# A fused attention and wave-MLP kernel: attention in fine stages, one written order for three batches

## The chip, the cores and the metric

One core of one Trainium2 chip. The metric is the device time of one execution in microseconds (us), as the median of the runs. Five engines work side by side, each on its own queue: TensorE (PE in the profile; PEld is its weight load), VectorE (DVE), ScalarE (ACT), GpSimd (POOL) and SyncE (SP), which here issues all the transfers.

## The reference

Eight batches, eight heads, 576 tokens, head size 64. First an attention in two parts, then a channel and token mixer on its output.

```python
q_d, k_d, v_d = (t.reshape(B, H, 144, 4, D).mean(axis=3) for t in (q, k, v))
out_up = np.repeat(softmax(q_d @ k_d.T / 8) @ v_d, 4, axis=2)      # pooled attention
scores = np.where(abs(pos[:, None] - pos[None, :]) < 4, q @ k.T / 8, -1e9)
out_local = softmax(scores) @ v                                     # band of seven tokens
x = (out_up + out_local).transpose(0, 2, 1, 3).reshape(B, 576, 512)

theta = x @ w_theta
y = einsum('ts,bsd->btd', w_tok_r, x * cos(theta)) + einsum('ts,bsd->btd', w_tok_i, x * sin(theta))
u = x + y
out = u + maximum(u @ w_ch, 0)
```

## The kernel before

All matmuls are in bf16 with float32 sums; the inputs arrive as float32 and are cast on the chip. The batches run one after another as a software pipeline written by hand. Every stage is a Python generator that emits a few instructions and then yields:

- `load(b)` (L78) issues the transfers of q, k and v on SP's queue, in pieces. `cast(b)` (L126) turns them into bf16, on GpSimd but for the first batch's queries. The float32 and the bf16 buffers exist once each, v in bf16 twice.
- `attention(b)` (L278) is one generator for the whole attention. Its eight turns (L294) bring q and k into the layout with the head dimension on partitions, one pair of heads at a time, with the pooling as 24 more columns of the same matmul; ScalarE copies the 576 turned columns and VectorE the 144 pooled ones. For the first two batches (`WIDE`) q and k arrive in another layout and a turn has twelve matmuls. Then come the pooled values (L336), three steps of pooled scores with their exponentials (L354), five steps of scores, each with an exponential on ScalarE and two masking passes on GpSimd (L388), two of pooled output (L423), mixed in among the scores, and five of output (L461). An output step upsamples the pooled result by a matmul with a staircase matrix (`RT`; two matmuls where a chunk of 120 tokens lies on the border of the two halves of 72 pooled rows, six in a batch), multiplies the masked scores with v, and makes a chunk of x on VectorE (reciprocal, product `tmp`, sum `x`).
- `modulate(b)` (L503) transposes x, multiplies by w_theta, takes cosine and sine on ScalarE (a table of its own, so the engine reloads its table twice a batch) and multiplies by x on VectorE (`z`).
- `mix(b)` (L545) has eight steps of token mix and five of channels. In the token mix the two halves of the 576 tokens are built side by side in two banks; after 20 matmuls VectorE adds x to both. A channel step multiplies by w_ch, transposes u back, applies the rectifier on ScalarE (`rel`), adds on VectorE (`osb`) and stores.
- `build_WT` (L241) loads, casts and transposes the two token matrices, within the first batches.

The order of the work comes from the string `PERIOD` (L610): in iteration b it takes steps of attention b+1 (a), modulation b (m) and mix b-1 (x) in turn. Each attention itself emits the loads and casts of the next batch (`next(loads, 0)`, `ahead()`). The first attention is emitted alone ahead of the loop. The framework that places the instructions may still reorder what is emitted within an engine, by priorities of its own; it also sets the semaphores.

PSUM has eight banks: tiles of two banks with two buffers (`w2`: turns, scores, pooled scores and outputs) and tiles of one bank with four (`w1`: pooled values, upsampling, transposes, phases, mix, channels).

Of the kernel before, what the change touches and what calls it, by code (L numbers as in the profile page):

```python
# [13 lines left out]
P = 128  # L14
# [31 lines left out]
def kernel(  # L46
# [31 lines left out]
    def load(b):  # L78

        ts = staged[b] = []  # L80
        for nm in "qk":
            ts.append(work.tile([TR, NTR * H * D], FP32, tag=f"{nm}32", bufs=1, name=f"{nm}32_{b}"))
        if b < WIDE:
            for hh in range(4):
                for t, src in zip(ts, (q, k)):
                    nc.sync.dma_start(
                        out=t.rearrange("p (h e) -> p h e", h=H)[:, 2 * hh:2 * hh + 2, :],
                        in_=src[b, 2 * hh:2 * hh + 2].rearrange("h (p r) d -> p h (r d)", r=NTR),
                    )
                    yield  # L90
        else:
            for t, src in zip(ts, (q, k)):
# [7 lines left out]
        t = work.tile([P, NCH, H, D], FP32, tag="v32", bufs=1, name=f"v32_{b}")  # L100
        ts.append(t)
# [21 lines left out]
    kdT = const.tile([P, 4, 180], BF16, name="kdT")  # L123
    nc.vector.memset(kdT[:, :, SD:180], 0.0)

    def cast(b, engines):  # L126

        q32, k32, v32 = staged.pop(b)
# [4 lines left out]
        if b < WIDE:  # L133
            for hh in range(4):
                for eng, dst, src in ((engines[0], q_tm, q32), (engines[1], k_tm, k32)):
                    eng(out=dst[:, :, 2 * hh:2 * hh + 2, :].rearrange("p r h d -> p h r d"),
                        in_=src.rearrange("p (h r d) -> p h r d", h=H, d=D)[:, 2 * hh:2 * hh + 2])
                    if hh % 2 == 0 or eng is engines[1]:
                        yield
        else:  # L140
            for eng, dst, src in ((engines[0], q_tm, q32), (engines[1], k_tm, k32)):
                for c in range(0, NTR, 2):
                    eng(out=dst[:, c:c + 2], in_=src.rearrange("p (c h d) -> p c h d", c=NTR, d=D)[:, c:c + 2])  # L143
                    yield
        engines[2](out=v_w[:, 0:2, :, 0:D], in_=v32[:, 0:2])
        yield
        engines[2](out=v_w[:, 2:4, :, 0:D], in_=v32[:, 2:4])
        yield
        engines[2](out=v_w[0:KW[4], 4, :, 0:D], in_=v32[0:KW[4], 4])
# [21 lines left out]
    pw = moep.tile([TR, NTR, SD], BF16, tag="rel", bufs=3, name="pw")  # L171
# [14 lines left out]
    for _ in range(6):  # L186
# [39 lines left out]
    for c in range(4):  # L226
# [3 lines left out]
    ru = const.tile([72, 288 + S], BF16, name="ru")  # L230
    nc.vector.memset(ru, 1.0)
    nc.gpsimd.affine_select(out=ru, in_=ru, compare_op=ALU.is_ge, fill=0.0,
                            base=-288, pattern=[[1, 288 + S]], channel_multiplier=-4)
    nc.gpsimd.affine_select(out=ru, in_=ru, compare_op=ALU.is_ge, fill=0.0,
                            base=291, pattern=[[-1, 288 + S]], channel_multiplier=4)
    RT = [ru[:, 288 - 288 * g:288 - 288 * g + S] for g in range(2)]
# [4 lines left out]
    def build_WT():  # L241
        w_tm = [moep.tile([P, 5, S], BF16, tag="uT", name=f"wtm{ri}") for ri in range(2)]
        pieces = []
        for ri, w_dram in enumerate((moe_w_tok_r, moe_w_tok_i)):
            for ct in range(5):
                t = moep.tile([P, S], FP32, tag=("osb", "rel")[ct % 2], bufs=3, name=f"wt32_{ri}{ct}")
                rows = OC[ct]
                nc.sync.dma_start(out=t[0:rows], in_=w_dram[P * ct:P * ct + rows, :])
                pieces.append((w_tm[ri][0:rows, ct, :], t[0:rows]))
                if len(pieces) == 5:  # L250
                    yield
                if len(pieces) > 5 or ri:
                    dst, src = pieces.pop(0)
                    nc.gpsimd.tensor_copy(out=dst, in_=src)
        nc.sync.dma_start(out=w32[1], in_=moe_w_ch.rearrange("(c p) e -> p c e", p=P))
        yield
        for dst, src in pieces:
            nc.gpsimd.tensor_copy(out=dst, in_=src)
            yield
        for c in range(4):  # L260
            nc.gpsimd.tensor_copy(out=wch[:, c, :], in_=w32[1][:, c, :])
# [12 lines left out]

    xs = {}


    def attention(b):  # L278
        q_tm, k_tm, v_w = inputs.pop(b)
        loads = load(b + 1) if b + 1 < B else iter(())  # L280
        casts = []

        def ahead(n=1):
            if b + 1 < B:
                if not casts:
                    casts.append(cast(b + 1, (nc.gpsimd.tensor_copy,) * 3))
                for _ in range(n):
                    next(casts[0], 0)

        qT = work.tile([P, 4, S], BF16, tag="qT", bufs=1, name=f"qT{b}")  # L290
        kT = work.tile([P, 4, S], BF16, tag="kT", bufs=1, name=f"kT{b}")
        qdT = work.tile([P, 4, SD], BF16, tag="qdT", bufs=1, name=f"qdT{b}")

        def turn(n, hh):  # L294
            tm, To, Tdo = ((q_tm, qT, qdT), (k_tm, kT, kdT))[n]
# [366 lines left out]
```

## Time and profile before

| what | value |
|---|---|
| median of 3 runs | 335.38 us (335.3 to 335.72) |
| the profiled execution | 336.12 us |
| its span, first to last instruction | 334.4 us |
| mean granted TensorE clock | 0.923 |
| busy: TensorE, weight loads | 294.0 us (88%), 204.9 us (61%) |
| busy: VectorE, ScalarE, GpSimd | 195.0, 186.0, 159.2 us (58, 56, 48%) |
| moved by DMA | 43.57 MB, mean 130 GB/s |

Busy times are sums of instructions' durations, overlaps counted once. A row of a timeline has a start, a length, an engine, a line of the kernel, an operation, what it writes and reads, how many instructions are merged, and in brackets the idle time before it with what ended it. Matmuls are pipelined: the length of a merged row runs past the start of the next one, so the cost of a group is read from one start to the next. The granted clock is given as a share of full speed, a mean over the stretch of the two levels 1.2 and 2.4 GHz.

### The profile page before, as it was taken

To read this page: it belongs to the slowest core of one execution; us is meant where nothing else is said; L and a number is where in the kernel's file an instruction comes from. 1 tells how busy PE (TensorE), PEld (TensorE's weight loads), DVE (VectorE), ACT (ScalarE), POOL (GpSimd) and SP (SyncE) were. 2 spreads that over 40 slices of the span, in tenths; PEclk is the share of its full clock that TensorE was granted. 3 is DMA by queue.
4 is the path that set the end of the run, shared out by engine and by line. 5 is a ranking of instruction groups with operands and counts; after the bars stand their busy time and mean duration, and the time that the engine had idled before them with its cause. 6 is when DMAs were issued, how large, how long until landed. Compare 5 with 4: busy or idle time off the path is not lost.

```text
span 334.4 us, 7314 instructions
## 1 busy us (share of the span) xinstructions
PE 294.0 (88%) x2940; PEld 204.9 (61%) x2954; DVE 195.0 (58%) x441; ACT 186.0 (56%) x280; POOL 159.2 (48%) x186
## 2 busy tenths in 40 slices
PE   1688898999996899979997899889998999699994
PEld 1664685576664676557664666566755766467672
DVE  5426846594546764685439664766466544934533
ACT  1264289424874668628872787377855596333302
POOL 6977504893049524964477447815790008300000
PEclk9995589558999999979999999999998999979999
DMA  8999999959302289639917895477012000300303
GB/s 221 235 321 218 234 285 228 200 92 201 77 2 90 62 142 206 143 104 204 194 38 212 153 209 101 142 176 142 2 65 78 2 0 14 117 16 2 136 7 141
DMA packets 107826, 43.57 MB, mean 130 GB/s; under 512 B 97424, under 2 KB 101520, under 8 KB 107792
## 3 DMA queue, kind: packets, MB, share of 16 engines
q1 hardware_dynamic: 107792, 43.10, 58.6%
q8 instruction: 23, 0.38, 0.5%
q14 instruction: 11, 0.09, 0.1%
HBM read 33.65 MB, written 9.44 MB: 129 GB/s over the span
## 4 chain that ended last, share of the span: by engine, by line
PE 39%; ACT 17%; POOL 13%; issue 12%; DVE 10%; DMA 5%; SPq 3%; POOLq 0%; DVEq 0%; ACTq 0%
PE psu L553 13%; PE psth L528 9%; POOL pm L414 4%; POOL pm L416 3%; DVE tmp L486 3%; DMA q<-in_q_dram 3%; ACT pd L367 3%; POOL k_tm L143 3%; PE psr L573 3%; PE pstr L314 2%; ACT pm L401 2%; DVE osb L600 2%; PE pstr L304 2%; PE psnd L428 2%; DVE x L493 2%
## 5 line engine op out<-in xcount | busy, mean ns | idle before, releaser
L553 PE MATMUL psu<-WT,z 120*128 120x288 bf16 (+1 forms) x640 | 92.3, 291 | 0.0
L553 PEld LDWEIGHTS <-z 120*128 120x128 bf16 (+1 forms) x640 | 60.3, 99 | 18.4 <-issue 0.2
L414 POOL TENSOR_SCALAR_AFFINE_SELECT pm<-pm 128x1024 bf16<-128x1024 bf16 (+1 forms) x32 | 33.4, 1052 | 56.0 <-ACT pm L401 52.9
L401 ACT ACTIVATE pm<-psS 128x1024 bf16<-128x1024 f32 (+1 forms) x40 | 38.6, 982 | 20.7 <-PE psS L393 18.7
L528 PE MATMUL psth<-wth,xT 128*120 128x512 bf16 (+1 forms) x160 | 45.1, 405 | 4.7 <-DVE xT L518 3.8
L598 ACT ACTIVATE rel<-psr 128x512 f32<-128x512 f32 (+1 forms) x40 | 22.4, 559 | 48.1 <-PE psr L573 38.6
L143 POOL CAST q_tm<-q 96x1024 bf16<-96x1024 f32 x18 | 22.6, 1276 | 46.4 <-PE pstr L314 21.0
L535 ACT ACTIVATE cs<-psth,pihc 120x512 bf16<-120x512 f32 (+1 forms) x40 | 27.5, 688 | 29.9 <-PE psth L528 29.8
L537 DVE TENSOR_TENSOR z<-cs,x 120x1024 bf16<-120x1024 bf16 (+1 forms) x40 | 32.5, 813 | 18.6 <-ACT cs L536 18.5
L562 DVE TENSOR_TENSOR uT<-psu,xT 128x288 bf16<-128x288 f32 x64 | 26.8, 452 | 28.0 <-PE psu L553 28.0
L325 ACT CAST qT<-pstr 128x576 bf16<-128x576 f32 x32 | 20.2, 642 | 36.7 <-PE pstr L314 21.3
L600 DVE TENSOR_TENSOR osb<-rel,psx 128x512 f32<-128x512 f32 (+1 forms) x40 | 25.2, 631 | 21.5 <-ACT rel L598 21.5
L416 POOL TENSOR_SCALAR_AFFINE_SELECT pm<-pm 128x1024 bf16<-128x1024 bf16 (+1 forms) x32 | 33.7, 1059 | 0.8
L573 PE MATMUL psr<-wch,uT 128*128 128x512 bf16 x114 | 31.2, 379 | 1.4 <-issue 0.9
L477 PEld LDWEIGHTS <-pm 128*128 128x128 bf16 (+1 forms) x320 | 16.5, 112 | 21.9 <-POOL pm L416 13.8
L528 PEld LDWEIGHTS <-xT 128*120 128x120 bf16 (+1 forms) x160 | 20.5, 139 | 14.1 <-DVE xT L518 4.8
L518 DVE COPY xT<-xTps 128x480 bf16<-128x480 bf16 (+1 forms) x40 | 15.5, 389 | 23.3 <-PE xTps L513 23.2
L477 PE MATMUL psloc<-v_w,pm 128*128 128x65 bf16 (+1 forms) x320 | 19.5, 209 | 9.3 <-POOL pm L416 5.7
L486 DVE TENSOR_TENSOR tmp<-psloc,rl 120x512 bf16<-120x512 f32 (+1 forms) x40 | 26.5, 683 | 0.0
L493 DVE TENSOR_TENSOR x<-tmp,psup 120x512 bf16<-120x512 bf16 (+1 forms) x40 | 26.4, 680 | 0.0
L143 POOL CAST k_tm<-k 96x1024 bf16<-96x1024 f32 x18 | 19.6, 1114 | 12.9 <-PE pstr L314 12.0
L536 ACT ACTIVATE cs<-psth 120x512 bf16<-120x512 f32 (+1 forms) x40 | 23.6, 590 | 0.0
(87 smaller groups left out, 457.1 us busy)
## 6 DMA issues: line engine op xcount, KB each, us to landing
v<-in_v_dram SPq DMA_DIRECT2D x32, 256.0 KB, 5.4
out_dram<-osb SPq DMA_DIRECT2D x32, 256.0 KB, 2.0
q<-in_q_dram SPq DMA_DIRECT2D x36, 192.0 KB, 4.0
k<-in_k_dram SPq DMA_DIRECT2D x36, 192.0 KB, 4.7
q<-in_q_dram SPq DMA_DIRECT2D x8, 288.0 KB, 5.1
k<-in_k_dram SPq DMA_DIRECT2D x8, 288.0 KB, 6.1
v<-in_v_dram SPq DMA_DIRECT2D x8, 200.0 KB
wt<-in_moe_w_tok_r_dram SPq DMA_DIRECT2D x4, 288.0 KB
```

Source lines behind the costliest of these rows:

```text
L143: eng(out=dst[:, c:c + 2], in_=src.rearrange("p (c h d) -> p c h d", c=NTR, d=D)[:, c:c + 2])
L401: nc.scalar.activation(out=pv, in_=ps[0:kw].rearrange("p e (j w) -> p (e j) w", w=P)[:, :, 0:qn], func=AF.Exp, scale=SCL,)
L414: nc.gpsimd.affine_select(out=pv, in_=pv, compare_op=ALU.is_ge, fill=0.0, base=off, pattern=[[0, 8], [-1, qn]], channel_multiplier=1)
L416: nc.gpsimd.affine_select(out=pv, in_=pv, compare_op=ALU.is_ge, fill=0.0, base=6 - off, pattern=[[0, 8], [1, qn]], channel_multiplier=-1)
L477: nc.tensor.matmul(out=pv[0:qn, par, j, :], lhsT=pms[c][0:kw, 4 * par + j, 0:qn], rhs=v_w[0:kw, c, 2 * j + par, 0:65], start=(j == 0), sto ...
L486: nc.vector.tensor_tensor(out=tmp[0:cnt].rearrange("p (j e d) -> p e j d", e=2, j=4), in0=pv[0:cnt, :, :, 0:D], in1=rl[0:cnt].unsqueeze(3) ...
L493: nc.vector.tensor_tensor(out=x[0:cnt], in0=tmp[0:cnt], in1=up[0:cnt], op=ALU.add)
L528: nc.tensor.matmul(out=th[0:cnt, :], lhsT=xT[:, dc, QS[c]:QS[c] + cnt], rhs=wth[:, dc, :], start=(dc == 0), stop=(dc == 3),)
L537: nc.vector.tensor_tensor(out=z[0:cnt, c, :, :], in0=cs[0:cnt], in1=xt[c][0:cnt].unsqueeze(1).to_broadcast([cnt, 2, DM]), op=ALU.mult,)
L553: nc.tensor.matmul(out=pss[hf][:, 0:288], lhsT=z[0:QC[c], c, ri, P * dc:P * dc + P], rhs=WT[0:QC[c], ri, c, 288 * hf:288 * hf + 288], star ...
L573: nc.tensor.matmul(out=psr, lhsT=uT[:, dc, P * c:P * c + P], rhs=wch[:, dc, :], start=(dc == 0), stop=(dc == 3),)
L600: nc.vector.tensor_tensor(out=osb[:, 0:w], in0=rel[:, 0:w], in1=psx[:, 0:w], op=ALU.add)
```

## The change

- The attention becomes four generators: `turns`, `scores`, `pooled_out`, `outputs`. `modulate` becomes `transposes`, `phases` and `modulate`; `mix` becomes `mix`, `channels` and `store`. `load` and `cast` are generators of the loop, no longer driven from inside the attention. Masks stay in `scores`.
- From batch 2 on a turn takes one chunk of 96 tokens for all heads (four matmuls, one bank) instead of all tokens of one head pair (six matmuls, two banks): twelve turns, not eight.
- `kdT`, `kT`, `qT` and `qdT` get two buffers each. A query or key buffer for the next load is taken when its load begins.
- The pooled output is made in two overlapping blocks of 120 rows, so that each upsampling is one matmul, five in a batch.
- The token mix fills one bank at a time, with ten matmuls and one eviction.
- The order is written out in five strings, one letter a step: `a` and `A` turns of batch 0 and of b+1, `S` scores, `N` pooled output, `V` outputs, `T` transposes, `H` phases, `Z` products of batch b, `X` mix, `R` channels, `O` stores of batch b-1, `C` casts of b+2, `L` loads of b+3, `W` the token matrices, `l`, `c`, `k` the loads and casts of batches 1 and 2 at the start. `FIRST` is iteration 0, `SECOND` 1, `PERIOD` 2 to 6, `LAST` 7, `END` 8.
- `pin` adds, after each step, an ordering edge without a semaphore from every instruction to the one emitted before it on its engine, so that the framework keeps the emitted order on each of them.

```diff
-    kdT = const.tile([P, 4, 180], BF16, name="kdT")
+    kdTs = []
+    for i in range(2):
+        t = const.tile([P, 4, 180], BF16, name=f"kdT{i}")
...
-    ru = const.tile([72, 288 + S], BF16, name="ru")
+    rt = const.tile([120, 488], BF16, name="rt")
...
+        def turn(n, c):
+            tm, To, Tdo = pairs[n]
+            ps = w1(f"pstr{n}{c}_{b}")[:, 0:4 * TW].rearrange("p (hh w) -> p hh w", w=TW)
+            for hh in range(4):
+                nc.tensor.matmul(
+                    out=ps[:, hh, :], lhsT=tm[:, c, 2 * hh:2 * hh + 2, :], rhs=ip, start=True, stop=True,
+                )
+            nc.scalar.copy(out=To[:, :, TR * c:TR * c + TR], in_=ps[:, :, 0:TR])
+            nc.vector.tensor_copy(out=Tdo[:, :, TP * c:TP * c + TP], in_=ps[:, :, TR:TW])
+
+        for i in range(8 if b < WIDE else 12):
             if b < WIDE:
-                turn(i % 2, i // 2)
+                wide_turn(i % 2, i // 2)
             else:
-                turn(i // 4, i % 4)
+                turn(i // 6, i % 6)
             yield
...
-                        out=pv[0:72, h // 4, h % 4, :],
-                        lhsT=pd[:, kk, h, 72 * g:72 * g + 72],
+                        out=pv[0:120, h // 4, h % 4, :],
+                        lhsT=pd[:, kk, h, 24 * g:24 * g + 120],
...
-            for g in range(g0, g1 + 1):
-                nc.tensor.matmul(
-                    out=up[0:qn, :],
-                    lhsT=RT[g][:, QS[c]:QS[c] + qn],
-                    rhs=xd[:, g, :],
-                    start=(g == g0), stop=(g == g1),
-                )
+            o = QS[c] - 96 * (c == 4)
+            nc.tensor.matmul(out=up[0:qn, :], lhsT=rt[:, o:o + qn], rhs=xd[:, c // 4, :], start=True, stop=True)
...
         for dc in range(4):
-            pss = [w1(f"psu{dc}{hf}_{b}") for hf in range(2)]
-            for c in range(NCH):
-                for ri in range(2):
-                    for hf in range(2):
+            for hf in range(2):
+                cols = slice(288 * hf, 288 * hf + 288)
+                ps = w1(f"psu{dc}{hf}_{b}")
+                for c in range(NCH):
+                    for ri in range(2):
                         nc.tensor.matmul(
-                            out=pss[hf][:, 0:288],
+                            out=ps[:, 0:288],
                             lhsT=z[0:QC[c], c, ri, P * dc:P * dc + P],
-                            rhs=WT[0:QC[c], ri, c, 288 * hf:288 * hf + 288],
+                            rhs=WT[0:QC[c], ri, c, cols],
                             start=(c == 0 and ri == 0), stop=(c == NCH - 1 and ri == 1),
                         )
-                if c == 2:
-                    yield
-            for hf in range(2):
-                nc.vector.tensor_tensor(
-                    out=uT[:, dc, 288 * hf:288 * hf + 288], in0=pss[hf][:, 0:288],
-                    in1=xT[:, dc, 288 * hf:288 * hf + 288], op=ALU.add,
-                )
-            yield
+                nc.vector.tensor_tensor(out=uT[:, dc, cols], in0=ps[:, 0:288], in1=xT[:, dc, cols], op=ALU.add)
+                yield
...
+    FIRST = (
+        "aWallaWaaalaSlllaWlaccSSNcWSWlcNSlcVSVlAlVcSAAcklTTlkkWVSWTAcAHWTVAHWcZHccWTkkZAkCckWkkkZCHWAkWCCWHC"
+        "WLLLCAZLLWLWWCCZCLWLLLL"
+    )
+    SECOND = (
+        "ASAXSAXSAXANSXAXAVASXSXSNTROSAACXRCAAOVRHOTVCVHLTVCRLHTZTCLCHZZHCLZRZOLOCCSLLLLL"
+    )
     PERIOD = (
-        "m a m a a x m a x m a a x m a x m a "
-        "a a x a a x a a x a a x a a x a x a a x a x a a x"
-    ).split()
+        "SSXXAXSAASAANXANASAAXVSAAXSTCVXASCCVHXCCTVROHTCVRLOHTRZHOTCCLLRLZOZZHCRZSOLLLLLL"
+    )
+    LAST = (
+        "SSXXXSSXNSXSVXSVTXSVRHONTXTVHVSHTRTZOZROHZHZZRORO"
+    )
+    END = (
+        "XXXXXXXROROXRORROO"
+    )
...
+    def pin():
+
+        ins = nc.cur_bb.bb.instructions
+        for i in range(done[0], len(ins)):
+            e = ins[i].engine
+            if e in last:
+                tc.add_manual_dep(ins[i], last[e], mybir.DependencyInfo(
+                    mybir.DependencyClass.NoSync, mybir.DependencyReason.DATA), reason="order")
+            last[e] = ins[i].name
+        done[0] = len(ins)
+
+    def run(order, **gens):
+        for s in order.replace(" ", "") + "".join(gens):
+            for _ in gens[s] if s in gens else ():
+                pin()
+                break
+        for s in gens:
+            for _ in gens[s]:
+                pin()
```

## Rows read from the trace of the kernel before

**Rows 1.** The page: engines' busy time, and the clock granted in 40 slices.

```profile
PE 294.0 (88%) x2940; PEld 204.9 (61%) x2954; DVE 195.0 (58%) x441; ACT 186.0 (56%) x280; POOL 159.2 (48%) x186
...
PEclk9995589558999999979999999999998999979999
```

**Rows 2.** Windows: four batches together, 126.96 to 271.21 us, and their mean.

```profile
sum 144.25, PE 132.43 PEld 90.86 DVE 88.83 ACT 93.46 POOL 76.51; mean PE 33.11 PEld 22.71 DVE 22.21 ACT 23.36 POOL 19.13
```

**Rows 3.** TensorE's timeline in one batch: start, length, line, operation, count.

```profile
205.00 0.40 PE L393 MATMUL psS<-qT,kT 64*128 64x128 bf16 x8
205.32 0.74 PE L428 MATMUL psnd<-vd,pd 90*72 90x65 bf16 x16
205.91 1.15 PE L553 MATMUL psu<-WT,z 120*128 120x288 bf16 x8
...
209.05 1.04 PE L573 MATMUL psr<-wch,uT 128*128 128x512 bf16 x4
209.92 0.39 PE L578 MATMUL psx<-ident,uT 128*128 128x128 bf16 x4
210.15 0.38 PE L467 MATMUL psup<-xd,ru 72*128 72x512 bf16 x1
210.37 0.41 PE L477 MATMUL psloc<-v_w,pm 128*128 128x65 bf16 x8
210.69 0.38 PE L467 MATMUL psup<-xd,ru 72*128 72x512 bf16 x1
...
229.25 0.34 PE L513 MATMUL xTps<-ident,x 96*128 96x96 bf16 x4
229.42 1.04 PE L528 MATMUL psth<-wth,xT 128*120 128x512 bf16 x4
230.29 0.48 PE L314 MATMUL pstr<-ip,k_tm 96*128 96x120 bf16 x6
230.61 1.15 PE L553 MATMUL psu<-WT,z 120*128 120x288 bf16 x8
231.60 1.03 PE L528 MATMUL psth<-wth,xT 128*96 128x512 bf16 x4
```

**Rows 4.** Windows: the end of that batch's attention (length, busy times, clock, DMA, GB/s).

```profile
212.00:222.00 10.00, 7.32 (x83) 4.83 (x83) 9.09 (x21) 4.17 (x7) 3.95 (x5) 1.00 0.67 179
```

**Rows 5.** TensorE's timeline: first pooled score of batch 1, first token mix.

```profile
52.63 0.39 PE L356 MATMUL psSd<-qdT,kdT 64*90 64x144 bf16 x6
...
78.33 1.76 PE L553 MATMUL psu<-WT,z 120*128 120x288 bf16 x12
```

**Rows 6.** Windows: the second batch's attention and the token matrices.

```profile
53.80:90.50 36.70, 34.18 (x306) 24.02 (x305) 22.93 (x54) 19.68 (x29) 18.97 (x22) 0.72 0.85 156
```

**Rows 7.** Groups by line and form: copies out of the turns (busy, mean ns).

```profile
L325 ACT CAST qT<-pstr 128x576 bf16<-128x576 f32 x32 | 20.2, 642 | 36.7 <-PE pstr L314 21.3 <-PE pstr L304 15.2
...
L326 DVE CAST qdT<-pstr 128x144 bf16<-128x144 f32 x32 | 9.1, 299 | 5.8 <-ACT qT L325 5.7
```

**Rows 8.** Groups by line and form: VectorE's work at a batch's end.

```profile
L600 DVE TENSOR_TENSOR osb<-rel,psx 128x512 f32<-128x512 f32 x32 | 21.9, 686 | 20.2 <-ACT rel L598 20.2
L486 DVE TENSOR_TENSOR tmp<-psloc,rl 120x512 bf16<-120x512 f32 x32 | 21.2, 685 | 0.0
...
L518 DVE COPY xT<-xTps 128x480 bf16<-128x480 bf16 x32 | 12.7, 399 | 23.3 <-PE xTps L513 23.2
```

**Rows 9.** z by tile (ns min/median/max), then VectorE's and GpSimd's timelines near 233.

```profile
L537 DVE TENSOR_TENSOR z<-cs,x x40: 681/692/1710, 45.7 to 306.2; 120x1024 bf16<-120x1024 bf16 x32, 96x1024 bf16<-96x1024 bf16 x8
...
233.86 1.71 DVE L537 TENSOR_TENSOR z<-cs,x 96x1024 bf16<-96x1024 bf16 x1 [0.52 <-ACT cs L536]
...
233.01 3.47 POOL L143 CAST k_tm<-k 96x1024 bf16<-96x1024 f32 x3 [2.76 <-PE pstr L314]
```

**Rows 10.** The transfers of the first 60 us.

```profile
DMA packets 26877, 14.87 MB, mean 248 GB/s; under 512 B 21624, under 2 KB 24696, under 8 KB 26872
```

**Rows 11.** VectorE's timeline at the end of the span.

```profile
329.62 1.09 DVE L600 TENSOR_TENSOR osb<-rel,psx 128x512 f32<-128x512 f32 x2 [0.40 <-ACT rel L598]
```

More of the change, by code (lines that the diff above doesn't have):

```diff
@@ L273, in build_WT @@
                 yield
[L275 to L295, printed above, removed]
-            ps = w2(f"pstr{n}{hh}_{b}")
-            if b < WIDE:
-                for r in range(NTR):
-                    nc.tensor.matmul(
-                        out=ps[:, r // 3, (r % 3) * TR:(r % 3) * TR + TR],
-                        lhsT=tm[:, r, 2 * hh:2 * hh + 2, :], rhs=ip[:, 0:TR], start=True, stop=True,
-                    )
-                for r in range(NTR):
-                    nc.tensor.matmul(
-                        out=ps[:, 0, 3 * TR:3 * TR + SD],
-                        lhsT=tm[:, r, 2 * hh:2 * hh + 2, :], rhs=pw[:, r, :],
-                        start=(r == 0), stop=(r == NTR - 1),
-                    )
-                src = ps[:, :, 0:3 * TR].rearrange("p k (c w) -> p w k c", w=TR)
-                dst = To[:, hh, :].rearrange("p (w k c) -> p w k c", k=2, c=3)
-                srcd, dstd = ps[:, 0, 3 * TR:3 * TR + SD], Tdo[:, hh, 0:SD]
-            else:
-                for c in range(NTR):
-                    nc.tensor.matmul(
-                        out=ps[:, c // 3, (c % 3) * TW:(c % 3) * TW + TW],
-                        lhsT=tm[:, c, 2 * hh:2 * hh + 2, :], rhs=ip, start=True, stop=True,
-                    )
-                pv = ps[:, :, 0:3 * TW].rearrange("p k (c w) -> p k c w", w=TW)
-                src, dst = pv[:, :, :, 0:TR], To[:, hh, :].rearrange("p (k c w) -> p k c w", k=2, c=3)
-                srcd, dstd = pv[:, :, :, TR:TW], Tdo[:, hh, 0:SD].rearrange("p (k c w) -> p k c w", k=2, c=3)
@@ L506, in modulate @@
         state[b] = (xT, z)
-        xt = xs.pop(b)
-        def transposes(c):
+        for c in range(NCH):
             cnt = QC[c]
@@ L598, in mix, with store @@
             nc.scalar.activation(out=rel[:, 0:w], in_=psr[:, 0:w], func=AF.Relu)
+            rels[b, c] = (rel, psx, w)
+            yield
+        state.pop(b)
+    def store(b):
+        for c in range(5):
+            rel, psx, w = rels.pop((b, c))
             osb = moep.tile([P, DM], FP32, tag="osb", bufs=3, name=f"osb{c}_{b}")
@@ new lines, in run @@
+    def run(order, **gens):
[6 more added lines that the diff above has]
+                pin()
+    gp = (nc.gpsimd.tensor_copy,) * 3
+    for b in range(B + 1):
+        gens = {}
+        if b == 0:
+            gens.update(a=turns(0), l=load(1), c=cast(1, gp), k=load(2), W=build_WT())
+        if b < B:
+            gens.update(S=scores(b), N=pooled_out(b), V=outputs(b), T=transposes(b), H=phases(b), Z=modulate(b))
+        if b + 1 < B:
+            gens["A"] = turns(b + 1)
+        if b + 2 < B:
+            gens["C"] = cast(b + 2, gp)
+        if b + 3 < B:
+            gens["L"] = load(b + 3)
+        if b:
+            gens.update(X=mix(b - 1), R=channels(b - 1), O=store(b - 1))
+        run({0: FIRST, 1: SECOND, B - 1: LAST, B: END}.get(b, PERIOD), **gens)
```

232 lines of the change are left out of this document (122 added, 110 removed).

## The prediction, made before the change was run

> **What bounds the kernel now.** I read the page's table of engines first, then the span cut at the repeating point of a batch, then TensorE's order of time within one batch, then the start. TensorE is the busiest engine, and its granted clock is near 1 except in the first quarter [rows 1]. Cut where ScalarE writes the pooled values, the span has four like batches of 144.25 us together, 36.06 us each; in the mean one TensorE is busy 33.1 us, VectorE 22.2, ScalarE 23.4, GpSimd 19.1 [rows 2]. Busy time of overlapping matmuls flatters, so I price a batch by distances between starts where TensorE runs without a gap at full clock [rows 3]: a token-mix matmul (X) takes 0.124 us (eight in 0.99), a phase step H 0.87, six turn matmuls (A) 0.32, a transpose step T 0.17, a channel step R 0.87 + 0.23 = 1.10, one upsampling matmul 0.22 and the eight of the local output 0.32, a score step 0.32, a pooled output N 0.59. A batch then holds 9.9 (80 X) + 4.35 (5 H) + 2.56 (48 A) + 1.09 (five 512-column matmuls for the pooled values, at H's rate) + 5.5 (5 R) + 2.92 (5 outputs V with six upsamplings) + 1.6 (5 scores) + 0.8 (16 pooled scores, at the scores' rate per column) + 1.18 (2 N) + 0.9 (5 T) = 30.8 us. So 36.06 - 30.8 = 5.3 us of each batch is not TensorE work at full clock. About half of it has a place: from 212 to 222 us VectorE is busy 9.09 of 10 and TensorE 7.32 [rows 4]. That is the end of one batch's attention: five outputs, stores and transposes queue on VectorE, the mix matmuls that could cover them are spent, and the next phases wait for the transposes. The start is the other loss: the first pooled score of batch 1 comes at 52.63 us and the first mix matmul at 78.33 [rows 5], at a granted clock of 0.72 over most of that stretch [rows 6].
>
> **The change, part by part.** *Upsampling* by one matmul a chunk takes six to five: -0.22 us a batch [rows 3], so 30.6. *Pooled output* with 120 weight columns for 72: the local output, with 128 weight columns and as many moving ones, takes 0.32/8 = 0.040 us a matmul against 0.59/16 = 0.037 [rows 3]; between nothing and 32 x 0.003 = 0.1 us, taken as nothing. *Mix by single banks*: still 80 matmuls and eight evictions a batch, only their order differs; nothing on TensorE, and it needs one of the four single banks at a time instead of two. *Turns* become twelve of four matmuls: TensorE the same. ScalarE copies 384 columns instead of 576, for which it takes 642 ns [rows 7]. Twelve pieces cost between 12 x 0.43 (pure columns) and 12 x 0.64, against 8 x 0.64 = 5.1 now: 0 to +2.6 us; I take +0.6, as most of such a copy is columns. VectorE's share goes from eight pieces of 299 ns [rows 7] to twelve smaller ones: 0 to +1.2 us, taken +0.6. Both engines have over 10 us free in a batch [rows 2], and double kT, qT and kdT let the turns run under the scores; without that cover these 1.2 us would stand in the scores' path.
>
> *The order.* In the repeating string, mix steps stand between pooled scores, turns, scores and the first three outputs; the last mix step comes before channel step 0. Outputs V2 to V4 stand among phases, channel steps and transposes, so VectorE's work is spread. From V2 to the end of the string VectorE has 3 outputs of two 0.685 us operations (the second, x, priced as tmp), 4 transposes of 0.40, 5 stores of 0.69 [rows 8] and 5 products z of 0.69 [rows 9]: 4.1 + 1.6 + 3.4 + 3.5 = 12.6 us (reciprocals and one mix eviction left out). TensorE in the same steps has 3 x 0.54 + 5 x 0.87 + 1.24 + 4 x 0.17 + 5 x 1.10 + 1.09 = 14.5 us. It fits, closely. The pins add no wait of their own, but each queue becomes strict. SP: the query load for batch b+3 stands between two stores; it waits for the casts that free its buffer, and the next store, the three output buffers, VectorE and the transposed banks of R queue behind it. By the string the casts are issued a few us of TensorE work earlier. GpSimd: the first cast stands before the last mask, and the fifth output waits for that mask; the distance is 6 us of TensorE work. The last stores stand ahead of seven of the loads; these have most of the next batch to land. I cost all three at nothing with that cover, and at a few tenths each without it.
>
> So a batch costs 30.6 + e. The bounds of e are 0 and today's 5.3. I take 1.8: the 2.7 us lost between 212 and 222 [rows 4] should mostly go, and of the other 2.6 (short waits, lapses of the clock) some two thirds stay.
>
> *The start.* The opening string does the work that now ends at 52.63, plus the 50 token-weight transposes, which stand after it now: 50 x 0.058 (0.23/4, [rows 3]) = 2.9 us, up to twice that at the lower clock. That puts the first mix step near 57 us. By bytes it could start earlier: 14.87 MB moved in the first 60 us, 0.248 MB/us [rows 10], and batches 0 and 1 with theta and both token matrices are 10.8 MB, about 44 us; then cast, turn and transpose, so 50 is the low end, and 72 the high one (today's 78.33 less part of the batch-1 attention already done there).
>
> **The sum.** 57 + six batches x 30.6 (183.6) + the last batch without turns 27.0 + the closing mix and channel steps 9.9 + 5.5 = 15.4 + the end, 334.4 - 329.62 = 4.8 [rows 11], + 7 x 1.8 = 12.6: 300.4 us of span. The same sum for the kernel before is 69 (78.3 less 9 us of work that the change does later) + 184.8 + 27.2 + 15.4 + 4.8 + 7 x 5.3 = 338, against 334.4: the method is good to some 4 us. The profiled execution took 336.12 us, 1.7 over its span; the median is 0.7 below it. So 300.4 + 1.7 - 0.7 = 301.4, given as 301.
>
> **The rivals.** (1) *VectorE becomes the bound.* z alone takes 0.69 us (the median), but 1.71 when it started during a GpSimd cast [rows 9]. The new order puts the value casts and the masks beside the z products. If each of five waits 1.0 us, VectorE's 12.6 becomes 17.6 against 14.5, and e grows by 3.1 to 4.9: 300.4 + 7 x 3.1 = 322 span, 323. If half do, 312. For it: rows 9; against: by the string only two of the z stand beside casts. The Trainium skill ("SBUF — State Buffer", Who interferes with whom) says that a VectorE instruction with two SBUF inputs and a GpSimd one that reads SBUF block each other; by that rule, and the 1.71 us agree, each z beside a cast or mask is held. Chance 0.2.
>
> (2) *The start stays long.* The opening string holds GpSimd in order: masks, casts and weight conversions cannot pass each other while data lands. If the first mix step comes at 72, it is 316. Chance 0.1.
>
> (3) *The clock; slower than before.* Strict order and one bank at a time make TensorE pause briefly before many groups, and the clock falls to 1.2 GHz for stretches. It is what 53.8 to 90.5 us show: 34.2 of 36.7 us busy, clock 0.72 [rows 6]. At a mean clock c a batch costs 30.6/c + 1.8; with the start and the end held as in the sum, it passes 334 where a batch passes 37.3, that is c below 0.87. At 0.72 throughout, a batch is 44 us and the whole 57 + 6 x 44 + 39 + 21 + 5, about 386. Against it: at those four batches the waits were longer than the string leaves, and the page's clock still was mostly 9 tenths [rows 1]. The Trainium skill ("TensorE: Matmul & The Clock Gate", A second HAM failure mode: psum-queue depth-cycling) says that cycling through banks makes short idles between groups that let the clock swing between its levels. That rule speaks against single banks and would give this rival. Chance 0.07.
>
> (4) *It does not do what it says.* If chains between engines and not the order set the 5.3 us, e stays, and only the start could gain; as the opening string then also pays, nothing within measurement changes: 335. Chance 0.03.
>
> **How the numbers follow.** Forecast 0.6, with e from 0.6 to 3 and a start of 53 to 62: 289 to 315. The range 288 to 322 adds most of rivals 1 and 2 and leaves out about 0.17. A measurement of this kernel tells about 0.2% from no change. Faster: 0.6 + 0.2 + 0.1 and a little of rival 4 = 0.91; same 0.02; slower 0.07.
>
> **What would show it.** Right: the cut at the pooled values repeats every 32 to 33 us with clock 1.00; the first mix matmul is near 57; the busiest ten-us stretch of VectorE no longer coincides with TensorE at 7 tenths; five upsamplings a batch. Rival 1: z's mean near 1 us or more and TensorE idle for osb or xT. Rival 2: first mix matmul after 65. Rival 3: clock digits of 5 to 8 beyond the start. I am wrong if a batch still takes over 35 us with z at 0.7 and the clock at 1.00: then a queue that I priced at nothing (stores behind loads, masks behind casts) is the wait.

## The result, and the profile after

The changed kernel takes 299.78 us (median of 4 runs, 298.93 to 302.53), beside 335.34 us for the kernel before on the same chip: a ratio of 0.896, with an interval of 0.890 to 0.903. The forecast was 301, the range 288 to 322. The profiled execution took 298.93 us, and its span is 297.2.

The first lines are the page of the changed kernel: busy times, the clock and TensorE in 40 slices, and the chain that ended last.

```profile
PE 275.5 (93%) x2946; PEld 197.4 (66%) x2946; DVE 204.1 (69%) x466; ACT 189.7 (64%) x304; POOL 159.5 (54%) x186
...
PE   2497899999989999999999999999999999999993
...
PEclk9998579999999999999999999999999999999999
...
PE 75%; DMA 7%; POOL 4%; SPq 4%; DVE 4%; ACT 2%; issue 1%; DVEq 0%; POOLq 0%; ACTq 0%
```

Against [rows 1] the clock no longer lapses after the first fifth of the span, and TensorE is at eight or nine tenths from the fifth slice to the last but one. The chain is three quarters TensorE; in the kernel before it was 39%:

```profile
PE 39%; ACT 17%; POOL 13%; issue 12%; DVE 10%; DMA 5%; SPq 3%; POOLq 0%; DVEq 0%; ACTq 0%
```

The second view cuts the span where the pooled values of a batch are copied, as [rows 2] did. Columns: stretch and length, then the busy time of TensorE, its weight loads, VectorE, ScalarE and GpSimd, each with its count, then the granted clock, the DMA share and GB/s.

```profile
55.71:91.80 36.09, 34.17 (x361) 23.22 (x361) 27.05 (x60) 24.21 (x40) 22.48 (x23) 1.00 1.20 206
91.80:123.80 32.00, 31.36 (x351) 22.46 (x351) 23.69 (x56) 23.73 (x39) 19.81 (x19) 1.00 0.76 161
...
155.14:186.48 31.34, 31.34 (x351) 22.39 (x351) 23.32 (x56) 23.71 (x40) 19.82 (x19) 1.00 0.77 155
...
249.16:297.20 48.04, 43.09 (x423) 30.22 (x422) 28.18 (x58) 21.78 (x33) 10.36 (x10) 1.00 0.17 56
76.00:91.80 15.80, 13.88 (x122) 8.03 (x120) 14.05 (x30) 9.98 (x19) 8.72 (x9) 1.00 1.14 218
155.14:171.00 15.86, 15.86 (x211) 12.40 (x211) 9.59 (x29) 12.72 (x22) 6.08 (x6) 1.00 1.14 207
171.00:186.48 15.48, 15.48 (x143) 9.99 (x141) 13.73 (x28) 10.99 (x19) 13.73 (x14) 1.00 0.39 101
```

Four batches in a row (one shown, 155 to 186 us) take 31.34 us each, to 0.01 us, and TensorE is busy in all of it: the list of its waits from 124 to 249 us is empty. The last two lines are the halves of one of them. In the second half VectorE is busy 13.73 of 15.48 us, nearly full as in [rows 4], but now TensorE has work under it. The stretch from 76 to 91.8 shows what that looks like without cover: VectorE 14.05 of 15.80, TensorE 13.88. `SECOND`, the string of that batch, has used up its mix steps by then (the last group starts at 74.77 us).

The third view is TensorE's timeline: token-weight transposes in the opening string, the first pooled score of batch 1 and the first mix matmul, then a pooled output and a local output of a later batch.

```profile
47.22 0.55 PE L278 MATMUL wps<-ident,wtm 128*120 128x128 bf16 x5
47.70 1.07 PE L517 MATMUL psth<-wth,xT 128*120 128x512 bf16 x4
...
57.50 0.39 PE L368 MATMUL psSd<-qdT,kdT 64*90 64x144 bf16 x6
...
58.04 1.39 PE L553 MATMUL psu<-WT,z 120*128 120x288 bf16 x10
...
161.63 1.02 PE L437 MATMUL psnd<-vd,pd 90*120 90x65 bf16 x16
162.48 1.39 PE L553 MATMUL psu<-WT,z 120*128 120x288 bf16 x10
...
172.81 0.41 PE L467 MATMUL psloc<-v_w,pm 128*128 128x65 bf16 x8
173.05 1.05 PE L517 MATMUL psth<-wth,xT 128*120 128x512 bf16 x4
```

The first pooled score of batch 1 comes later than before, at 57.50 us for 52.63 [rows 5], but the first mix matmul follows at once, at 58.04 for 78.33. In `90*120` the second number is the columns of weights. From start to start a pooled output takes 0.85 us for 16 matmuls with 120 columns of weights, against 0.59 with 72 [rows 3]; a local output, with 128 columns, takes 0.24 for eight. Five token-weight transposes, again with 120 columns, take 0.48.

The fourth view is the groups by line and form (busy us, mean ns), two of them weight loads, and z by tile (ns min/median/max):

```profile
L334 ACT CAST kT<-pstr 128x384 bf16<-128x384 f32 x36 | 16.0, 483 | 9.8 <-PE pstr L331 9.8
...
L335 DVE CAST qdT<-pstr 128x96 bf16<-128x96 f32 x36 | 9.2, 256 | 16.1 <-ACT qT L334 14.8
...
L524 ACT ACT_TABLE_LOAD x8 | 10.3, 1283 | 3.0 <-PE psth L517 2.9
...
L379 ACT ACT_TABLE_LOAD x7 | 9.0, 1283 | 0.1
...
L437 PEld LDWEIGHTS <-pd 90*120 90x120 bf16 x256 | 16.3, 140 | 2.2 <-issue 1.0 <-DVE xd L445 0.9
...
L467 PEld LDWEIGHTS <-pm 128*128 128x128 bf16 x256 | 12.4, 100 | 6.2 <-DVE tmp L476 1.9 <-DVE xd L445 0.4 <-issue 0.3
```

```profile
L533 DVE TENSOR_TENSOR z<-cs,x x40: 676/684/1458, 48.2 to 277.0; 120x1024 bf16<-120x1024 bf16 x32, 96x1024 bf16<-96x1024 bf16 x8
```

### The profile page after: what moved, and what is told of

Its sections match the earlier page's. It is cut to its first block, busy times and chain, and to the rows that moved or that the text cites. A ratio compares the mean times of both kernels' runs of the same rounds, so it can differ in the third digit from the quotient of the medians.

```text
span 297.2 us, 7393 instructions
## 1 busy us (share of the span) xinstructions
PE 275.5 (93%) x2946; PEld 197.4 (66%) x2946; DVE 204.1 (69%) x466; ACT 189.7 (64%) x304; POOL 159.5 (54%) x186
## 4 chain that ended last, share of the span: by engine, by line
PE 75%; DMA 7%; POOL 4%; SPq 4%; DVE 4%; ACT 2%; issue 1%; DVEq 0%; POOLq 0%; ACTq 0%
PE psu L553 26%; PE psth L517 11%; PE psr L573 8%; PE pstr L331 6%; PE psnd L437 4%; PE psS L400 3%; DMA q<-in_q_dram 3%; PE psvd L349 3%; SPq L107 3%; PE psloc L467 3%; PE psup L462 3%; PE xTps L500 2%; DMA w<-in_moe_w_theta_dram 2%; PE psx L578 2%; PE psSd L368 2%
## 5 line engine op out<-in xcount | busy, mean ns | idle before, releaser
L553 PE MATMUL psu<-WT,z 120*128 120x288 bf16 (+1 forms) x640 | 87.0, 286 | 0.2 <-ACT rel L598 0.2
L559 DVE TENSOR_TENSOR uT<-psu,xT 128x288 bf16<-128x288 f32 x64 | 29.0, 454 | 26.2 <-PE psu L553 25.9
L517 PE MATMUL psth<-wth,xT 128*120 128x512 bf16 (+1 forms) x160 | 41.3, 381 | 0.2 <-DVE xT L505 0.2
L524 ACT ACTIVATE cs<-psth,pihc 120x512 bf16<-120x512 f32 (+1 forms) x40 | 27.4, 686 | 16.0 <-PE psth L517 13.8
L573 PE MATMUL psr<-wch,uT 128*128 128x512 bf16 x128 | 33.0, 378 | 0.0
L533 DVE TENSOR_TENSOR z<-cs,x 120x1024 bf16<-120x1024 bf16 (+1 forms) x40 | 29.2, 756 | 0.8 <-ACT cs L525 0.8
L517 PEld LDWEIGHTS <-xT 128*120 128x120 bf16 (+1 forms) x160 | 18.0, 131 | 7.9 <-DVE xT L505 0.7
L153 POOL CAST v_w<-v 128x1024 bf16<-128x1024 f32 x16 | 18.4, 1166 | 7.7 <-DMA v<-in_v_dram 5.2
L334 ACT CAST kT<-pstr 128x384 bf16<-128x384 f32 x36 | 16.0, 483 | 9.8 <-PE pstr L331 9.8
L335 DVE CAST qdT<-pstr 128x96 bf16<-128x96 f32 x36 | 9.2, 256 | 16.1 <-ACT qT L334 14.8
L334 ACT CAST qT<-pstr 128x384 bf16<-128x384 f32 x36 | 16.2, 484 | 4.9 <-PE pstr L331 4.9
```

What stands on the lines that cost most here:

```text
L334: nc.scalar.copy(out=To[:, :, TR * c:TR * c + TR], in_=ps[:, :, 0:TR])
L517: nc.tensor.matmul(out=th[0:cnt, :], lhsT=xT[:, dc, QS[c]:QS[c] + cnt], rhs=wth[:, dc, :], start=(dc == 0), stop=(dc == 3),)
L524: nc.scalar.activation(out=cs[0:cnt, 0, :], in_=th[0:cnt], func=AF.Sin, bias=pihc[0:cnt], scale=1.0)
L533: nc.vector.tensor_tensor(out=z[0:cnt, c, :, :], in0=css.pop((b, c))[0:cnt], in1=xs[b][c][0:cnt].unsqueeze(1).to_broadcast([cnt, 2, DM]), ...
L553: nc.tensor.matmul(out=ps[:, 0:288], lhsT=z[0:QC[c], c, ri, P * dc:P * dc + P], rhs=WT[0:QC[c], ri, c, cols], start=(c == 0 and ri == 0), ...
L559: nc.vector.tensor_tensor(out=uT[:, dc, cols], in0=ps[:, 0:288], in1=xT[:, dc, cols], op=ALU.add)
```

## The experiments

Each kernel is the changed one with one edit, except the second, and was run beside the kernel before on the same chip. Ratios are to that; the changed kernel's is 0.896.

### The ordering edges

```diff
 def pin():
-            if e in last:
+            if False:
```

> The changed kernel without the ordering edges: the same strings, but the framework may place each engine's instructions by its own priorities. Theory A (the written strings carry the gain; the edges only keep what is emitted): 298 to 307 us, a batch near 31.3 to 32.5. Rival B (the edges carry it, because the framework's own placement undoes a fine order): over 315 us, with gaps on TensorE as in the kernel before.

Measured: 343.05 us, ratio 1.020 (1.014 to 1.027). The strings are as in the changed kernel, the framework may reorder each engine, and not only is the whole gain gone, it is slower than before, by 1.4 to 2.7%. The window of one batch, the chain, two groups, and timelines from the batch after that one:

```profile
141.11:181.68 40.57, 35.36 (x349) 24.89 (x351) 26.45 (x55) 25.79 (x41) 20.25 (x20) 0.93 0.57 111
```

```profile
PE 62%; ACT 15%; issue 8%; DVE 8%; DMA 3%; SPq 1%; POOL 1%; DVEq 0%; POOLq 0%
```

```profile
L524 ACT ACT_TABLE_LOAD x16 | 20.5, 1283 | 2.7 <-DVE z L533 1.4 <-PE psth L517 1.1
L379 ACT ACT_TABLE_LOAD x13 | 16.7, 1283 | 0.2
```

```profile
200.81 1.03 POOL L149 CAST k_tm<-k 96x1024 bf16<-96x1024 f32 x1
201.80 0.88 POOL L423 TENSOR_SCALAR_AFFINE_SELECT pm<-pm 100x768 bf16<-100x768 bf16 x1
202.62 1.03 POOL L149 CAST k_tm<-k 96x1024 bf16<-96x1024 f32 x1
203.60 2.48 POOL L153 CAST v_w<-v 128x1024 bf16<-128x1024 f32 x2
...
201.51 3.67 DVE L533 TENSOR_TENSOR z<-cs,x 120x1024 bf16<-120x1024 bf16 x1
...
205.84 0.42 PE L462 MATMUL psup<-xd,rt 120*96 120x512 bf16 x1 [2.79 <-DVE x L483]
...
210.06 1.28 ACT L379 ACT_TABLE_LOAD   x1
...
212.75 1.28 ACT L524 ACT_TABLE_LOAD   x1
```

Three things are to be read there. ScalarE does an exponential of the pooled scores (L379) between two cosines (L524), and loads its table for each: 34 loads in the span (29 in these two groups) against 16 (15 in the two groups above), or 18 x 1.283 = 23 us more on that engine, whose share of the chain goes from 2% to 15%. A z stands beside five GpSimd operations in a row (the last row above holds two) and takes 3.67 us; x waits behind it, and TensorE for x, 2.79 us. And the clock is 0.93 in the batch from 141 to 182 us; in the batch of the timelines it is 1.00. How the 43 us divide among the three stays open.

Then the edges without the strings: `pin` after each step of the kernel before, whose own string stays.

```diff
             if g is not None:
                 next(g, 0)
+                pin()
```

> The kernel before with the same ordering edges added, its own string unchanged. Theory A: the coarse string stays the bound, 330 to 345 us. Rival B: below 322 us, since the edges would be what helps.

Measured: 359.13 us, ratio 1.064 (1.056 to 1.072). That is slower than either theory had it. Edges alone cost 22 us: the coarse string was better off with the framework's reordering. Which waits the edges add was not taken apart. So neither half alone, the strings or the edges, gains anything.

The next three free one engine each from the edges and leave the others fixed (shown for VectorE; `Activation` and `PE` stand there in the other two).

```diff
-            if e in last:
+            if e in last and e != mybir.EngineType.DVE:
```

> The changed kernel with the edges on every engine but VectorE. Without any edge the time was 343 us, with one z product of 3.67 us beside a row of casts and masks. Theory J (most of what the edges hold is VectorE's order: z late, after the casts): 315 to 340 us, z's longest over 3 us. Rival K (another engine's order, or all together): 298 to 306 us.

> The changed kernel with the edges on every engine but ScalarE. Without any edge there were 34 table loads of 1.28 us instead of 16. Theory L (ScalarE's order matters most: pooled exponentials hoisted among the sines): over 24 table loads and 306 to 330 us. Rival: 16 to 20 loads and 298 to 304 us, since a ScalarE that follows a pinned TensorE has little to choose from.

> The changed kernel with the edges on every engine but TensorE. Theory M (TensorE's order decides: pooled scores of the next batch and mix matmuls are drawn forward and are missing later): 306 to 335 us. Rival: 298 to 304 us.

Measured: VectorE free 311.01 us (ratio 0.929, 0.923 to 0.934); ScalarE free 299.34 (0.895); TensorE free 300.75 (0.898). Of the three, only VectorE's own edges are worth something, 11 us, which lies between the two expectations: the first mix matmul came at 62.4 instead of 58.04, and the six batches add up to 6.4 us more than in the changed kernel. The mechanism that I had written down for it does not hold: the longest z is 1.23 us, and its mean 801 ns against 756. In its six batches TensorE waits 1.7 us for x and 3.5 for `cs`; so the order of VectorE's queue costs it, but by which step is not shown. With ScalarE alone free there are still 16 table loads, and from the third batch on the batches take 32.00 and 31.34 us, as in the changed kernel. One of these three freed costs 0 to 11 us, all engines freed 43; GpSimd and SP were not freed alone, so whether the rest comes from them or from several queues drifting together is open.

### VectorE's work spread over the batch

```diff
-        "SSXXAXSAASAANXANASAAXVSAAXSTCVXASCCVHXCCTVROHTCVRLOHTRZHOTCCLLRLZOZZHCRZSOLLLLLL"
+        "SSXXAXSAASAANXANASAAXSAAXSCXASCCXCCVVTVHTVROHTCVRLOHTRZHOTCCLLRLZOZZHCRZSOLLLLLL"
```

> The changed kernel with one thing moved in the string of batches 2 to 6: outputs V0 to V2, transpose T0 and phase H0 come after the last mix step instead of among the mix steps. Theory A (a batch is short because mix work covers the outputs' work on VectorE): after the last mix step VectorE has 5 outputs (6.9), 5 transposes (2.0), 5 stores (3.2), 5 products (3.7) and reciprocals (0.9), 16.7 us, against 14.6 of TensorE, so a batch grows by 2 to 4 us and the whole, with five such batches, to 310 to 320 us, TensorE again idle for x and xT. Rival C (every engine has slack within a batch, so the place inside it does not matter): 299 to 303 us.

Measured: 319.05 us, ratio 0.948 (0.943 to 0.952), as expected. The first three outputs, with the first transpose and the first phase, are moved behind the last mix step, as in the kernel before. Windows of one batch and of five us in it, and two of TensorE's waits in the whole span (sum, times, longest):

```profile
163.51:198.49 34.98, 31.71 (x349) 22.43 (x351) 23.25 (x56) 23.59 (x40) 18.76 (x19) 1.00 0.72 139
183.00:188.00 5.00, 3.48 (x37) 2.34 (x39) 4.83 (x11) 1.53 (x2) 4.93 (x6) 1.00 0.00 0
```

```profile
PE xTps L500 <- DVE x L483: 7.5, 8, 1.3
PE psth L517 <- DVE xT L505: 5.2, 5, 1.0
```

The batch grows by 3.6 us at the same clock, and TensorE idles for 3.3 of it, most of it where five outputs queue: transposes wait for x, phases for the transposed x. In the five us shown VectorE is busy 4.83 and TensorE 3.48, the picture of [rows 4].

The last experiment on this puts the five z earlier, three of them where GpSimd casts and masks (one store and one phase also change places):

```diff
-        "SSXXAXSAASAANXANASAAXVSAAXSTCVXASCCVHXCCTVROHTCVRLOHTRZHOTCCLLRLZOZZHCRZSOLLLLLL"
+        "SSXXAXSAASAANXANASAAXVSAAXSTCVXASCCVHXCCTZVROHTZCVRLOHTZROHTZCCLLRLOHCZRSOLLLLLL"
```

> The changed kernel with each z product, in batches 2 to 6, placed soon after its phase step, all edges kept. Moving the casts' letters among z left GpSimd's times as they were, so this moves VectorE instead: the first z now come while GpSimd casts (173 to 185 us in the batch from 155 to 186). Theory A' (the late place of z is what keeps the two engines apart): z at 1.2 to 2 us in the mean, a batch 1 to 4 us longer, 305 to 320 us. Rival F (the hold falls into VectorE's free time): 298 to 303 us.

Measured: 305.07 us, ratio 0.912 (0.906 to 0.918), a batch of 32.57 against 31.34. The time lies at the lower edge of what was expected, but z is held far less than that theory had it. In the batch from 157 to 190 us the three z that start while GpSimd works take 0.90, 1.02 and 1.02 us, where the changed kernel has one of 1.04 in a batch; the longest of all takes 1.23, and the mean is 789 ns against 756:

```profile
181.57 1.02 DVE L533 TENSOR_TENSOR z<-cs,x 120x1024 bf16<-120x1024 bf16 x1
```

This one starts 0.57 us into three casts of 3.47 us together. The five z take some 0.6 us more than those of the changed kernel's batch. TensorE then waits 0.4 us at a time for x, which now stands behind a z; how much of that is the hold and how much the place of z is not separated.

A try to bring the casts beside the z from the other side, by writing the `C` letters among the `Z`:

```diff
-        "SSXXAXSAASAANXANASAAXVSAAXSTCVXASCCVHXCCTVROHTCVRLOHTRZHOTCCLLRLZOZZHCRZSOLLLLLL"
+        "SSXXAXSAASAANXANASAAXVSAAXSTVXASVHXTVROHTVROHTRZCHOTCRCZCOCZCZCHCRZCSOLLLLLLLLLL"
```

> The changed kernel with all nine casts of batches 2 to 6 moved among the z products at the end of the string, the loads behind them. Theory A' (VectorE and GpSimd hold each other up when z meets a cast; in the changed kernel VectorE is busy 13.73 of the last 15.48 us of a batch, so it has 1.75 us to give): five z at 1.0 to 2 us more, a batch 2 to 4 us longer, 310 to 322 us, z's mean over 1.2 us. Rival F (the hold is short or falls into idle time): 299 to 303 us, z's mean under 0.9.

Measured: 299.86 us, ratio 0.893 (0.888 to 0.898). The theory failed, but the edit didn't do what it was for: GpSimd made its casts from 175.83 us on to 185.25, where it makes them from 173.63 to 184.88 in the changed kernel. With the order on GpSimd fixed by the edges, a letter sets the rank of a step and not its time. One z in a batch takes 1.60 us there, and the batch still takes 31.34: a hold of 0.9 us costs nothing in that place. For five held z it shows nothing.

### Banks

The old token mix, two banks side by side (with one `X` moved earlier in three of the other strings, so that every eviction stands before its reader):

```diff
-            for hf in range(2):
...
-                ps = w1(f"psu{dc}{hf}_{b}")
...
+            pss = [w1(f"psu{dc}{hf}_{b}") for hf in range(2)]
```

> The changed kernel with the old token mix: two banks side by side, 20 matmuls, then two evictions (in the second, the last and the closing string one mix step stands earlier, since a half step leaves nothing to go on with). Theory A prices single banks at nothing: 298 to 303 us, a batch at 31.3 to 31.7. Rival D (four single banks are too few when mix holds two of them for two steps, and turns, transposes and upsampling wait for one): 1 to 2 us a batch, 307 to 315 us, with waits of turns or mix matmuls for a bank's reader.

Measured: 317.69 us, ratio 0.943 (0.938 to 0.949). I had priced this edit at nothing; it is 18 us (16 by the ratios), above the rival's range too. The window of one batch, and waits of TensorE in the whole span:

```profile
163.93:198.16 34.23, 32.16 (x349) 22.56 (x351) 23.82 (x56) 23.79 (x40) 19.32 (x19) 1.00 0.75 142
```

```profile
PE pstr L331 <- DVE x L483: 5.5, 5, 1.1
...
PE pstr L331 <- DVE qdT L335: 2.7, 5, 0.5
```

All engines do the same work at the same clock, and a batch takes 2.9 us more: a turn now waits for VectorE to have read x, that is, to let go of the bank of an upsampling, or for the copy of an earlier turn. With two of the four single banks held by the mix through a whole group of 20 matmuls, the others run out; that these waits end with VectorE's reading of a bank is what the rows show.

The old turns, eight of six matmuls in two-bank tiles (the strings stay; the four last `A` then find nothing to do):

```diff
-            ps = w1(f"pstr{n}{c}_{b}")[:, 0:4 * TW].rearrange("p (hh w) -> p hh w", w=TW)
+            ps = w2(f"pstr{n}{hh}_{b}")
...
-        for i in range(8 if b < WIDE else 12):
+        for i in range(8):
```

> The changed kernel with the old turns for batches 2 to 7: eight of six matmuls into a two-bank tile, in place of twelve of four into one bank; the strings as they are (the letters left over do nothing). Theory A (turns then compete with scores, pooled outputs and outputs for the two two-bank tiles, and each holds one until a 642 ns copy is done): 1 to 3 us a batch, 306 to 318 us. Rival E (the same matmuls and fewer copies; the size of a turn does not matter): 297 to 302 us.

Measured: 342.22 us, ratio 1.020 (1.013 to 1.028): the direction is as expected, the size is two to seven times as large (42 us over the changed kernel, where 6 to 18 were expected). Windows of two batches and of a part of the first, and TensorE's timeline in the first:

```profile
153.00:192.94 39.94, 37.63 (x351) 25.84 (x351) 23.83 (x50) 23.86 (x36) 19.75 (x20) 0.84 0.61 121
192.94:231.98 39.04, 36.31 (x351) 24.32 (x352) 23.75 (x50) 23.91 (x36) 19.79 (x20) 0.89 0.60 124
183.00:196.00 13.00, 12.54 (x83) 8.56 (x83) 3.48 (x9) 4.19 (x7) 3.44 (x4) 0.50 0.73 114
```

```profile
179.61 0.48 PE L331 MATMUL pstr<-ip,q_tm 96*128 96x120 bf16 x6 [0.32 <-ACT pd L391]
180.48 0.40 PE L403 MATMUL psS<-qT,kT 64*128 64x128 bf16 x8 [0.39 <-DVE qdT L337]
181.16 0.48 PE L331 MATMUL pstr<-ip,q_tm 96*128 96x120 bf16 x6 [0.28 <-DVE qdT L337]
182.05 0.47 PE L331 MATMUL pstr<-ip,k_tm 96*128 96x120 bf16 x6 [0.42 <-ACT pm L411]
182.93 1.72 PE L440 MATMUL psnd<-vd,pd 90*120 90x65 bf16 x16 [0.40 <-DVE qdT L337]
184.45 2.59 PE L556 MATMUL psu<-WT,z 120*128 120x288 bf16 x10
...
197.19 1.03 PE L556 MATMUL psu<-WT,z 120*128 120x288 bf16 x7
```

Turns, scores and pooled outputs now share the two two-bank tiles, and each waits 0.3 to 0.4 us for the copy or the exponential of the one before. These gaps are small; what follows is not: ten mix matmuls in 2.59 us at 184.45, against 1.39 in the changed kernel. From 183 to 196 us the granted clock is 0.50, the lower level of 1.2 GHz; at 197.19 seven mix matmuls take 1.03 and it is back. In the first batch the gaps are 39.94 - 37.63 = 2.3 us, and the work of 31.34 us at a clock of 0.84 makes 37.3, which is the busy time. So some 6 of the 8.6 us lost there are clock and 2.3 are gaps.

### The start

All but the first of the token-matrix steps moved to the end of `FIRST`:

```diff
-    FIRST = (
-        "aWallaWaaalaSlllaWlaccSSNcWSWlcNSlcVSVlAlVcSAAcklTTlkkWVSWTAcAHWTVAHWcZHccWTkkZAkCckWkkkZCHWAkWCCWHC"
-        "WLLLCAZLLWLWWCCZCLWLLLL"
-    )
+    FIRST = "aWallaaaalaSlllalaccSSNcSlcNSlcVSVlAlVcSAAcklTTlkkVSTAcAHTVAHcZHccTkkZAkCckkkkZCHAkCCHCLLLCAZLLLCCZCLLLLLWWWWWWWWWWWWWWWWWW"
```

> The changed kernel with the steps of the token matrices, but for the first, moved to the end of the opening string. Theory A (the start is short because their loads, casts and 50 transposes stand inside the attention of batches 0 and 1): first mix matmul from 58 to 64 to 70 us, 305 to 313 us. Rival I (the transfers set the start and the transposes are hidden anyway): 298 to 302 us.

Measured: 332.0 us, ratio 0.989 (0.983 to 0.995), first mix matmul at 88.3. TensorE's timeline shows why it is more than expected:

```profile
62.61 0.36 PE L278 MATMUL wps<-ident,wtm 128*120 128x128 bf16 x1 [10.85 <-POOL wtm L259]
...
80.17 0.36 PE L278 MATMUL wps<-ident,wtm 128*120 128x128 bf16 x1 [11.18 <-POOL wtm L259]
```

These steps hold first fetches, then casts on GpSimd, then transposes, so that put together at the end they run one after another, with TensorE idle for 11 us twice. The second time it waits for a cast that had itself waited 13.85 us for its transfer, and the granted clock from 60 to 90 us is 0.50. Later batches again take 31.34 us, so the price of the start comes on top of the total in full.

The second batch by the repeating string (`SECOND` left out):

```diff
-        run({0: FIRST, 1: SECOND, B - 1: LAST, B: END}.get(b, PERIOD), **gens)
+        run({0: FIRST, B - 1: LAST, B: END}.get(b, PERIOD), **gens)
```

> The changed kernel with the string of batches 2 to 6 used for batch 1 too. The batch from 55.71 to 91.80 us takes 36.1 there against 31.3 later. Theory G (its own string spends the mix steps early, and from 77 us on the outputs, stores and transposes wait on VectorE): 32 to 34 us for that batch, 295.5 to 298.5 us in all. Rival H (the late landing of batch 2's keys and the masks behind their casts set it): 299 to 303 us.

Measured: 298.64 us, ratio 0.890 (0.883 to 0.896), beside 0.896 (0.890 to 0.903): the intervals overlap, and it can't be told from the changed kernel. In its profile that batch takes 34.6 us instead of 36.1, but its first mix matmul comes at 61.7 instead of 58.04. Theory G's bounds, 34 and 298.5 us, are just missed. What the batch gains there, the start has lost; the median lies 1.1 us lower, within the spread of the runs.

## Why the prediction was right or wrong

**The sum.** Forecast: 57 to the first mix matmul, 6 x (30.6 + 1.8) = 194.4, and 27.0 + 15.4 + 4.8 + 1.8 = 49.0 behind it. Measured by the cut: 55.7, then 36.1 + 32.0 + 4 x 31.34 = 193.5, then 48.0, which makes 297.2. Each of the three terms is within 2.5%. The cut lies 2.3 us ahead of the first mix matmul; counted from that matmul, as the forecast was, the terms are 58.0, 192.1 and 47.1, within 4%.

**The start** held: 58.04 against 57, well under the 72 of rival 2. The 50 token-weight transposes ahead of it take 5.0 us of TensorE between 44.45 and 57.19 us, within the 2.9 to 5.8 given for them, but at clock 1.00 from 45 us on: 0.10 us each and not the 0.058 read from transposes with 128 columns of weights.

**Spreading VectorE** held, and the third experiment shows it: with three outputs put back behind the mix, 3.6 us a batch return and the picture of [rows 4] comes again. My count of VectorE after V2, 12.6 against 14.5 us of TensorE, said that it fits closely; 13.73 of 15.48 us in the second half of a batch agree.

**The step of 1.8 us for what is lost, e, failed.** I took two thirds of 2.6 us to stay, as short waits and lapses of the clock. Of these nothing stays in the four like batches: no wait, and clock 1.00. The 31.34 - 30.6 = 0.74 us beyond the work are work, and most of that is a term that I had costed at nothing: the pooled output with 120 weight columns, at 0.855 us for 0.59, twice a batch, 0.53 us. I had bounded it by 0.1 from the local output with 128 weight columns at 0.040 us a matmul, as if 120 columns could not be dearer than 128; here they took 0.053. The rows, all with 65 moving columns, give 0.037 a matmul for 72 columns of weights, 0.053 for 120, and 0.030 to 0.040 for 128. The transposes differ in little but the weights: four with 128 columns take 0.23 us [rows 3], five with 120 take 0.48. A weight load lasts 140 ns in the mean in the pooled output and 100 in the local one. The Trainium skill ("TensorE: Matmul & The Clock Gate", Weight-path perf modes — Fast Weight Load (FWL) and DoubleRow) says that weights load fast where there are 128 of them; the rows agree with that, but no run here changed the width alone.

That the six batches came out near the sum all the same is partly luck. The second batch has 5.5 us over 30.6 (1.9 us of it TensorE idle, under a full VectorE, and 1.0 the last token-weight transposes), so that the errors cancel: 6 x 1.8 = 10.8 forecast, 5.5 + 1.4 + 4 x 0.74 = 9.9 measured. The sign that I gave for being right, a cut that repeats every 32 to 33 us, was missed on the short side, at 31.34.

**"Mix by single banks: nothing" and "turns: nothing" failed**, in what they would cost when undone: 18 and 42 us. I counted instructions and copies; those counts were right (384 columns take 483 ns, for which the 0.43 to 0.64 gave about 0.48, and VectorE's piece 256). What I did not count is how long a step holds a bank, and who needs that bank next. So the fine stages are no detail beside the order; with this order, undoing either of them gives back half of the gain or all of it.

**"The pins add no wait of their own"** was right for this order (on the coarse string they cost 22 us), and its converse was missed: I priced the queues as if the strings alone set the order. Without the edges the strings give 343 us, slower than before. My rival 4 (the order does nothing) fell, but a kernel with the order and without the edges would have been it, and worse. The SP and GpSimd queues, which I costed at nothing, show nothing in the four like batches: no wait of TensorE between 124 and 249 us.

**Rival 1** (z held beside GpSimd): a z takes up to 1.46 us after, with a median of 0.684 and a mean of 0.756, so some z are longer beside GpSimd, but with few of them it stays under TensorE's cover. The rule of the Trainium skill ("SBUF — State Buffer", Who interferes with whom), that a VectorE instruction with two SBUF inputs contends with a GpSimd instruction that reads SBUF, agrees with the 3.67 us of the first experiment, the longest hold here. Where I tried to provoke it with the order of z and casts, it came as 0.2 to 0.3 us on each of three z, and as 0.9 on one z a batch, where rival 1 had 1.0 us on all five; the batch grew by 1.2 us at most.

**Rival 3** (short pauses, clock at 1.2 GHz) isn't in the changed kernel, but its mechanism is in the coarse turns: 0.84 to 0.89 in two batches, and slower than before, near the break-even point of the forecast (a batch of 37.3 us is a clock of 30.6 / 35.5 = 0.86; I had written 0.87). The Trainium skill ("TensorE: Matmul & The Clock Gate", A second HAM failure mode: psum-queue depth-cycling) describes such gaps from cycling through banks. By that I held it against the single banks; the runs show the reverse, gaps where the tiles are large and two, none where they are small and four.

Not tried: the upsampling with five matmuls by itself (0.22 us a batch by the forecast, too little beside the interval), and the pooled output with 72 columns of weights in the new order. No experiment gave a kernel that is clearly faster than the changed one.

## What to carry to other kernels

Price a finer step not only by its instructions but by the banks that it holds and for how long: here two edits that leave every engine's work nearly as it was, priced at nothing, were worth 18 and 42 us. A written order and the edges that keep it are one change; either alone lost against the kernel before (343 and 359 us beside 337). Look first at the queue that is fullest where the bound engine idles, and give the bound engine work of another batch under it.

## What the runs showed of the hardware that was not expected

- Gaps of 0.28 to 0.42 us on TensorE, five within 3.7 us, were followed by 13 us at a granted clock of 0.50. Over the batch the gaps cost 2.3 us and the clock behind them 6.
- A z of 0.69 us took 3.67 beside five GpSimd operations that ran without a pause, and another 3.55 in the batch before, far above the 1.71 of [rows 9]. In the experiment with z early, a z begun within a cast took 0.90 to 1.02.
- A matmul with 120 columns of weights was dearer than one with 128, 0.053 us against 0.030 to 0.040, both with 65 moving columns, and a transpose 0.10 against 0.058. A pad of the pooled weights to 128 columns was not tried.
